# Attention step by step of one 128-query tile, with the exponentials left in PSUM

## The chip, the cores and the metric

One core of one Trainium2 chip runs the whole program. The metric is device time in microseconds; three runs of the kernel before gave a median of 1089.35 us.

## The reference

Three layers follow each other on a batch of 4 sequences of 576 tokens: attention with rotary embedding (8 heads of 64), a gated two-matrix block, and a token and channel mixer.

```python
q_rot, k_rot = (rotate(q), rotate(k))
scores = scale * np.matmul(q_rot, k_rot.transpose(0, 1, 3, 2))
scores = scores - np.max(scores, axis=-1, keepdims=True)
attn = np.exp(scores)
attn = attn / (np.sum(attn, axis=-1, keepdims=True) + 1e-09)
x = np.matmul(attn, v)
...
xk = mu_k * x + (1.0 - mu_k) * x_prev
xr = mu_r * x + (1.0 - mu_r) * x_prev
k = np.maximum(xk @ w_k, 0.0)
x = sigmoid(xr @ w_r) * (k * k @ w_v)
...
u = x + (np.maximum(x.T @ w_tok1, 0.0) @ w_tok2).T
out = u + np.maximum(u @ w_ch1, 0.0) @ w_ch2
```

## The kernel before

**Attention.** The 32 heads are worked on as 16 pairs. Of a pair, head 0 lies on partitions 0 to 63 and head 1 on 64 to 127. The 576 queries are four tiles of 128 and a last one of 64, which takes both heads at once; so a pair has nine score tiles of 128 queries by 576 keys, and the program 144. Float32 operands are split in a high and a low part, and a product is three matmuls; the keys come in two halves of 288, so a score tile is six matmuls (`emit_S`, tile `S`, two PSUM banks). VectorE takes the negative maximum (`emit_max`, `nm`), ScalarE the exponential into SBUF with the row sum (`emit_exp`, `e`), ScalarE adds the epsilon (`emit_den`, `den`), VectorE takes the reciprocal (`emit_rc`, `rc`), ScalarE writes the normalised probabilities in float16 (`emit_hi`, written by the helper `copy`, line 75, `p`), VectorE the float16 remainder (`emit_lo`, line 415), and a transposing DMA turns both into `pt` (`emit_tr`). `emit_pv` multiplies them with the split values (`pv`, 28 matmuls for each of two units of a pair), and ScalarE writes the result to `xT`.

**Steps.** `a_step(j)` runs one of five steps of a pair (`ND`), a step being a 128-query tile of both heads. It works on the exponentials of step j, the scores of j + 1 and the remainders of j - 1. In between, `other()` advances a second stream, `kvr_gen`, which computes the second layer's K and V products (`kp` in groups of 12 matmuls, `vp` in groups of 24, by `mm3`, lines 550 to 552), and `prep` rotates, splits and loads the next pair. During the first four pairs `Conv` converts weights in place of `kvr_gen`.

**Order and buffers.** What the code issues is put in order for each engine by a scheduler that follows priorities (`PRI`) and, through a timing model of its own, when operands and buffers come free; each engine then works strictly in that order. PSUM has eight banks: two score tiles of two banks (`S_p`), two banks for `pv` and the small products `vps` (`pv_p`), two for `kp` and `vp` (`acc_p`).

```python
S_p = ps.enter_context(tc.tile_pool(name="S_p", bufs=2, space=PS))
pv_p = ps.enter_context(tc.tile_pool(name="pv_p", bufs=2, space=PS))
acc_p = ps.enter_context(tc.tile_pool(name="acc_p", bufs=2, space=PS))
```

After attention the rest of the second layer, the token mixer (`trp`, `t1p`, `t2p`) and the channel mixer (`c1p`, `co`) follow.

## Time and profile before

| | before |
|---|---|
| median of 3 runs (lowest, highest) | 1089.35 us (1085.3, 1095.28) |
| the profiled execution | 1092.93 us |
| its span, first to last instruction | 1091.2 us |
| busy PE, DVE, ACT, POOL | 90%, 58%, 47%, 38% |
[...]

PE is TensorE, DVE VectorE, ACT ScalarE, POOL GpSimd. The busy shares are means over stretches with different limits, so the rows below split the span: scores run from 14 to 541 us, the last `pv` at 561 us, the channel mixer from 673 us on.

### The profile page before, as it was taken

To read this page: it belongs to the slowest core of one execution; us is meant where nothing else is said; L and a number is where in the kernel's file an instruction comes from. 1 tells how busy PE (TensorE), PEld (TensorE's weight loads), DVE (VectorE), ACT (ScalarE), POOL (GpSimd) and SP (SyncE) were. 2 spreads that over 40 slices of the span, in tenths; PEclk is the share of its full clock that TensorE was granted. 3 is DMA by queue.
4 is the path that set the end of the run, shared out by engine and by line. 5 is a ranking of instruction groups with operands and counts; after the bars stand their busy time and mean duration, and the time that the engine had idled before them with its cause. 6 is when DMAs were issued, how large, how long until landed. Compare 5 with 4: busy or idle time off the path is not lost.

```text
span 1091.2 us, 17428 instructions
## 1 busy us (share of the span) xinstructions
PE 980.3 (90%) x6544; PEld 859.3 (79%) x6544; DVE 636.8 (58%) x1098; ACT 510.2 (47%) x1160; POOL 411.9 (38%) x384
## 2 busy tenths in 40 slices
PE   2555877999999999999988799879999999999998
PEld 1443656878778777876587799879999999999998
DVE  6999986869878666761389448983223312232121
ACT  3656766767667565772455345444114212321110
POOL 5243354746758454330066355553014102201010
PEclk9955677989999999995779899889999999999999
DMA  6988698688878768573481025502021002000000
GB/s 204 251 235 168 145 192 165 151 169 172 179 157 161 166 131 157 114 163 60 97 244 70 22 61 200 230 12 55 1 66 45 23 1 65 7 22 1 23 22 22
DMA packets 212052, 120.77 MB, mean 111 GB/s; under 512 B 175232, under 2 KB 192768, under 8 KB 211840
## 3 DMA queue, kind: packets, MB, share of 16 engines
q1 hardware_dynamic: 211968, 119.67, 46.3%
q8 instruction: 51, 0.84, 0.3%
q14 instruction: 33, 0.27, 0.1%
HBM read 60.90 MB, written 14.16 MB: 69 GB/s over the span
## 4 chain that ended last, share of the span: by engine, by line
PE 67%; DVE 19%; issue 5%; DMA 4%; ACT 2%; POOL 2%; SPq 0%; DVEq 0%; POOLq 0%; ACTq 0%
PE S L368 9%; PE pv L444 6%; PE co L552 4%; PE c1p L550 4%; PE co L550 4%; PE co L551 4%; PE c1p L552 4%; PE c1p L551 4%; DVE p L415 4%; PE kp L550 4%; DVE cv L201 3%; PE kp L552 3%; PE kp L551 3%; PE vp L550 3%; PE vp L551 3%
## 5 line engine op out<-in xcount | busy, mean ns | idle before, releaser
L368 PE MATMUL S<-kq 64*128 64x288 f32 (+1 forms) x864 | 179.2, 356 | 52.8 <-ACT e L385 50.3
L368 PEld LDWEIGHTS S<-kq 64*128 64x128 f32 (+1 forms) x864 | 138.0, 221 | 85.8 <-ACT e L385 58.9
L415 DVE SCALAR_TENSOR_TENSOR p<-e,rc,p 128x576 f16<-128x576 f32 x144 | 149.2, 1058 | 23.7 <-ACT p L75 22.0
L376 DVE TENSOR_REDUCE nm<-S 128x1 f32<-128x576 f32 x144 | 107.4, 749 | 74.8 <-PE S L368 74.4
L385 ACT ACTIVATE e<-S,nm 128x576 f32<-128x576 f32 x144 | 105.8, 735 | 81.2 <-DVE nm L376 80.6
L880 DVE SCALAR_TENSOR_TENSOR hs<-c1p,hs 128x288 fp32r<-128x288 f32 x96 | 43.6, 454 | 151.3 <-ACT hs L879 151.0
L550 PE MATMUL c1p<-uhl,parts 128*128 128x288 f32 x384 | 116.5, 304 | 4.4 <-DVE hs L880 4.4
L879 ACT ACTIVATE hs<-c1p 128x288 fp32r<-128x288 f32 x96 | 38.7, 409 | 166.6 <-PE c1p L552 163.0
L551 PE MATMUL c1p<-uhl,parts 128*128 128x288 f32 x384 | 115.2, 300 | 0.0
L552 PE MATMUL c1p<-uhl,parts 128*128 128x288 f32 x384 | 114.7, 300 | 0.0
L75 ACT ACTIVATE p<-e,rc 128x576 f16<-128x576 f32 x144 | 104.1, 766 | 20.5 <-DVE rc L401 18.0
L552 PE MATMUL co<-hs,parts 128*128 128x288 f32 x384 | 113.0, 297 | 0.0
L551 PE MATMUL co<-hs,parts 128*128 128x288 f32 x384 | 113.0, 297 | 0.0
L550 PE MATMUL co<-hs,parts 128*128 128x288 f32 x384 | 109.4, 300 | 1.5 <-ACT hs L879 0.8
L104 POOL TENSOR_TENSOR k<-q,k 128x288 fp32r<-128x288 f32 x64 | 60.1, 943 | 114.6 <-DVE k L80 54.3
L104 POOL TENSOR_TENSOR uhl<-y,uhl 128x288 fp32r<-128x288 f32 x32 | 25.8, 838 | 195.2 <-ACT uhl L73 195.2
L550 PE MATMUL vp<-k,parts 128*128 128x288 f32 x256 | 84.1, 332 | 5.9 <-ACT vt L73 2.9
L444 PE MATMUL pv<-pt,vh 128*64 128x256 f16 (+1 forms) x576 | 76.4, 341 | 12.4 <-DMA pt<-p 10.7
L550 PE MATMUL kp<-xs,parts 128*128 128x288 f32 x256 | 84.8, 336 | 1.9 <-ACT t L611 1.3
L551 PE MATMUL vp<-k,parts 128*128 128x288 f32 x256 | 83.2, 326 | 0.0
L552 PE MATMUL vp<-k,parts 128*128 128x288 f32 x256 | 82.2, 322 | 0.0
L551 PE MATMUL kp<-xs,parts 128*128 128x288 f32 x256 | 81.4, 319 | 0.8 <-POOL xs L104 0.8
(113 smaller groups left out, 2409.0 us busy)
## 6 DMA issues: line engine op xcount, KB each, us to landing
words<-in_w_c_dram SPq DMA_DIRECT2D x24, 512.0 KB, 7.8
rq<-in_qin_dram SPq DMA_DIRECT2D x32, 320.0 KB, 3.3
rk<-in_kin_dram SPq DMA_DIRECT2D x32, 288.0 KB, 3.3
vr<-in_vw_dram SPq DMA_DIRECT2D x16, 320.0 KB, 3.1
xd<-xT SPq DMA_DIRECT2D x16, 288.5 KB, 2.5
vd<-vt SPq DMA_DIRECT2D x32, 144.0 KB, 2.2
y<-vd SPq DMA_DIRECT2D x8, 576.0 KB, 5.2
out_dram<-y SPq DMA_DIRECT2D x8, 576.0 KB, 3.5
```

Source lines behind the costliest of these rows:

```text
L75: act.activation(out=o, in_=i, func=AF.Copy, scale=scale)
L104: return (pool if e == "P" else dve).tensor_tensor(o, a, b, op=op)
L368: pe.matmul(ps[x][:, h, 0:HS], lhsT=a[l, 128 * m:128 * m + 128], rhs=b[l, h * HS:(h + 1) * HS], start=(n == 0), stop=(n == 2))
L376: dve.tensor_reduce(out=nm[:, x:x + 1], in_=p[:, :, 0:HS], op=ALU.max, axis=AX.XY, negate=True)
L385: act.activation(out=e, in_=p[:, :, 0:HS], func=AF.Exp, bias=sum_t[j][:, x:x + 1], accum_out=s[:, x:x + 1])
L415: dve.scalar_tensor_tensor(out=t[:, S:2 * S], in0=e_t[j][x], scalar=sum_t[j][:, x:x + 1], in1=t[:, 0:S], op0=ALU.mult, op1=ALU.subtract)
L444: pe.matmul(p[l, 0:n], lhsT=v[:, a, l], rhs=ts[x][:, c, :], start=(i == 0), stop=(i == len(prods) - 1))
L550: pe.matmul(p, lhsT=wh, rhs=t[:, 0], start=first, stop=False)
L551: pe.matmul(p, lhsT=wh, rhs=t[:, 1], start=False, stop=False)
L552: pe.matmul(p, lhsT=wl, rhs=t[:, 0], start=False, stop=last)
L879: act.activation(out=h[:, 0], in_=p[:, 0:HS], func=AF.Relu)
L880: dve.scalar_tensor_tensor(out=h[:, 1], in0=p[:, 0:HS], scalar=0.0, in1=h[:, 0].bitcast(F32), op0=ALU.max, op1=ALU.subtract)
```

## The change

A step is now one score tile instead of two heads' tiles: `ND` is 9, and the loop in `emit_S` over both heads is gone. The exponential overwrites the scores in PSUM, its row sum goes into a spare column of the same bank, and the tile stays taken until `emit_lo` has read it; before, it was free after `emit_exp`. The SBUF tile `e` and the ScalarE step `emit_den` go; VectorE adds the epsilon in a `tensor_scalar` ahead of the reciprocal. PSUM is now three score tiles, one bank for `pv` and `vps`, and one for `kp` and `vp`; only after attention (`second`) does `accps` also lend score tiles to these products. The raw loads `rk` and `rq` have four buffers instead of two, and the parts of `prep` and the `Conv` steps lie at other steps.

```diff
-ND = 5
-
-PV_AT = {4: 0, 6: 1}
+ND = 9
+
+PV_AT = {7: 0, 12: 1}
...
-BUFS = dict(rk=2, rq=2, sp=2, vr=2, v16=2, e=5, p16=4, pt=2, sm=4, sc=3, la=1, lf=1, xs=4, t=2, q=2, vt=2)
+BUFS = dict(rk=4, rq=4, sp=2, vr=2, v16=2, p16=4, pt=2, sm=4, sc=3, la=1, lf=1, xs=4, t=2, q=2, vt=2)
...
-        S_p = ps.enter_context(tc.tile_pool(name="S_p", bufs=2, space=PS))
-        pv_p = ps.enter_context(tc.tile_pool(name="pv_p", bufs=2, space=PS))
-        acc_p = ps.enter_context(tc.tile_pool(name="acc_p", bufs=2, space=PS))
+        S_p = ps.enter_context(tc.tile_pool(name="S_p", bufs=3, space=PS))
+        pv_p = ps.enter_context(tc.tile_pool(name="pv_p", bufs=1, space=PS))
+        acc_p = ps.enter_context(tc.tile_pool(name="acc_p", bufs=1, space=PS))
...
         @prio("S")
         def emit_S(j):
-            g, m = divmod(j, ND)
+            g, r = divmod(j, ND)
             (kh, kl), (qh, ql) = spl_t[g]
-            w = heads(j)
-            ps = [S_p.tile([128, 2, 512], F32, tag="S", name="S") for _ in range(w)]
+            m, x = divmod(r, 2)
+            l = slice(0, 128) if r == ND - 1 else slice(64 * x, 64 * x + 64)
+            p = S_t[j] = S_p.tile([128, 2, 512], F32, tag="S", name="S")
             for h in range(2):
                 for n, (a, b) in enumerate(((qh, kh), (qh, kl), (ql, kh))):
-                    for x in range(w):
-                        l = slice(64 * x, 64 * x + 64) if w == 2 else slice(0, 128)
-                        pe.matmul(ps[x][:, h, 0:HS], lhsT=a[l, 128 * m:128 * m + 128],
-                                  rhs=b[l, h * HS:(h + 1) * HS], start=(n == 0), stop=(n == 2))
-            S_t[j] = ps
+                    pe.matmul(p[:, h, 0:HS], lhsT=a[l, 128 * m:128 * m + 128], rhs=b[l, h * HS:(h + 1) * HS],
+                              start=(n == 0), stop=(n == 2))
...
         @prio("exp")
         def emit_exp(j):
-            s = sm_p.tile([128, 2], F32, tag="sum", name="sum")
-            e_t[j] = []
-            for x, p in enumerate(S_t.pop(j)):
-                e = e_p.tile([128, 2, HS], F32, tag="e", name="e")
-                act.activation(out=e, in_=p[:, :, 0:HS], func=AF.Exp, bias=sum_t[j][:, x:x + 1],
-                               accum_out=s[:, x:x + 1])
-                e_t[j].append(e.rearrange("p a b -> p (a b)"))
+
+            s = S_t[j][:, 0, HS:HS + 1]
+            e = S_t[j][:, :, 0:HS]
+            act.activation(out=e, in_=e, func=AF.Exp, bias=sum_t[j], accum_out=s)
             sum_t[j] = s
-
-        @prio("den")
-        def emit_den(j):
-            d = sm_p.tile([128, 2], F32, tag="den", name="den")
-            w = heads(j)
-            act.activation(out=d[:, 0:w], in_=sum_t[j][:, 0:w], func=AF.Identity, bias=eps, scale=1.0 / PSCALE)
-            sum_t[j] = d
 
         @prio("den")
         def emit_rc(j):
-            r = sm_p.tile([128, 2], F32, tag="rc", name="rc")
-            w = heads(j)
-            dve.reciprocal(r[:, 0:w], sum_t[j][:, 0:w])
+            r = sm_p.tile([128, 1], F32, tag="rc", name="rc")
+            d = sm_p.tile([128, 1], F32, tag="den", name="den")
+            dve.tensor_scalar(out=d, in0=sum_t[j], scalar1=1e-9, scalar2=1.0 / PSCALE, op0=ALU.add, op1=ALU.mult)
+            dve.reciprocal(r, d)
             sum_t[j] = r
 
         @prio("hi")
         def emit_hi(j):
-            p16_t[j] = []
-            for x, e in enumerate(e_t[j]):
-                t = p16_p.tile([128, 2 * S], F16, tag="p16", name="p16")
-                copy("A", t[:, 0:S], e, sum_t[j][:, x:x + 1])
-                p16_t[j].append(t)
+            t = p16_t[j] = p16_p.tile([128, 2, 2, HS], F16, tag="p16", name="p16")
+            copy("A", t[:, 0], S_t[j][:, :, 0:HS], sum_t[j])
 
         @prio("lo")
-        def emit_lo(j, x):
-            t = p16_t[j][x]
-            dve.scalar_tensor_tensor(out=t[:, S:2 * S], in0=e_t[j][x], scalar=sum_t[j][:, x:x + 1], in1=t[:, 0:S],
+        def emit_lo(j):
+            t = p16_t[j]
+            dve.scalar_tensor_tensor(out=t[:, 1], in0=S_t.pop(j)[:, :, 0:HS], scalar=sum_t[j], in1=t[:, 0],
                                      op0=ALU.mult, op1=ALU.subtract)
...
-            if k == -1:
+            if k == -2:
                 for n in range(3):
                     rope(g, 0, n, "DDP"[n] if g <= NP else "P")
                 ld_v(g + 1)
+            elif k == -1:
                 v_row(g)
             elif k == 0:
                 rope(g, 1, 0, "P")
@@ -474,21 +455,24 @@
                 split_hi(g, 0, "A")
                 v_pow(g)
             elif k == 1:
-                rope(g, 1, 2, "P")
-                split_lo(g, 0, "P")
                 v_all(g)
                 v_sc(g)
                 ld_raw(g + 1, 0, 0)
                 ld_raw(g + 1, 0, 1)
             elif k == 2:
+                rope(g, 1, 2, "P")
+                split_lo(g, 0, "P")
+            elif k == 3:
+                ld_raw(g + 1, 1, 0)
+                ld_raw(g + 1, 1, 1)
+            elif k == 4:
                 split_hi(g, 1, "A")
                 split_lo(g, 1, "D")
                 v_hi(g)
-                ld_raw(g + 1, 1, 0)
-                ld_raw(g + 1, 1, 1)
-            elif k == 3:
+            elif k == 5:
                 v_lo(g)
                 v_shift(g)
+            elif k == 6:
                 v_max(g + 1) if g + 1 < NG else None
...
             if j < NTT:
                 emit_exp(j)
             if j + 1 < NTT:
-                emit_S(j + 1)
+                emit_max(j + 1)
             other()
-            if j < NTT:
-                emit_den(j)
-            if j + 1 < NTT:
-                emit_max(j + 1)
             if j < NTT:
                 emit_rc(j)
                 emit_hi(j)
-            other()
             for gg in (g, g - 1):
                 r = j - gg * ND
                 if 0 <= gg < NG and r in PV_AT:
                     after.setdefault(j + 1, []).append(emit_pv(gg, PV_AT[r]))
             if 0 <= j - 1 < NTT:
-                for x in range(heads(j - 1)):
-                    emit_lo(j - 1, x)
-                    emit_tr(j - 1, x)
-                    other()
+                emit_lo(j - 1)
+                emit_tr(j - 1)
+            other()
+            if j + 2 < NTT:
+                emit_S(j + 2)
...
+
+        def accps(nm):
+            n_acc[0] += 1
+            if second and n_acc[0] % 4:
+                return S_p.tile([128, 2, 512], F32, tag="S", name=nm)[:, 0]
+            return acc_p.tile([128, 512], F32, tag="acc", name=nm)
+
+        n_acc = [0]
...
-                        p = acc_p.tile([128, 512], F32, tag="acc", name="kp")
+                        p = accps("kp")
...
-            if not cv.done() and j % 5 in (0, 2, 4):
+            if not cv.done() and j % 3 == 0:
...
-            if tps_n[0] % 3:
+            if tps_n[0] % 4:
```

The changed program orders the instructions anew. On PE, late in attention, the scores of the tile before the last pair stand among the `vp` products of the second stream. Before:

```order
L368 MATMUL S<-kq 128x288
L550 MATMUL vp<-k_5370,parts 128x288
L368 MATMUL S<-kq 128x288
L551 MATMUL vp<-k_5370,parts 128x288
L368 MATMUL S<-kq 128x288
L552 MATMUL vp<-k_5370,parts 128x288
L550 MATMUL vp<-k_5399,parts 128x288
L368 MATMUL S<-kq 128x288
L551 MATMUL vp<-k_5399,parts 128x288
L552 MATMUL vp<-k_5399,parts 128x288
L550 MATMUL vp<-k_5069,parts 128x288
```

The same place in the changed kernel:

```order
L532 MATMUL vp<-k_5378,parts 128x288
L530 MATMUL vp<-k_5422,parts 128x288
L531 MATMUL vp<-k_5422,parts 128x288
L532 MATMUL vp<-k_5422,parts 128x288
L362 MATMUL S<-kq 128x288 x18
L530 MATMUL vp<-k_5131,parts 128x288
L531 MATMUL vp<-k_5131,parts 128x288
L532 MATMUL vp<-k_5131,parts 128x288
L530 MATMUL vp<-k_5163,parts 128x288
```

The score matmuls stood one by one between single `vp` matmuls; now they stand in blocks of six or a multiple, between whole groups.

On DVE, in the middle of attention, `nm` is the maximum, `p` the remainder, `sc`, `vl`, `vm` and `kq` belong to the next pair, `f` and `k` to the second stream. Before:

```order
L415 SCALAR_TENSOR_TENSOR p_2383<-e,rc,p_2383 128x576
L540 SCALAR_TENSOR_TENSOR f<-xT,mu_s,a 128x288
L376 TENSOR_REDUCE nm<-S 128x1
L415 SCALAR_TENSOR_TENSOR p_2385<-e,rc,p_2385 128x576
L401 RECIPROCAL rc<-den 128x2
L376 TENSOR_REDUCE nm<-S 128x1
L342 SCALAR_TENSOR_TENSOR vl<-vr,sc,vh 128x640
L540 SCALAR_TENSOR_TENSOR f<-xT,mu_s,a 128x288
L415 SCALAR_TENSOR_TENSOR p_2469<-e,rc,p_2469 128x576
L415 SCALAR_TENSOR_TENSOR p_2471<-e,rc,p_2471 128x576
L376 TENSOR_REDUCE nm<-S 128x1
```

A like stretch in the changed kernel:

```order
L368 TENSOR_REDUCE nm<-S 128x1 x3
L382 TENSOR_SCALAR den<-S 128x1 x2
L383 RECIPROCAL rc<-den 128x1 x2
L382 TENSOR_SCALAR den<-S 128x1
L383 RECIPROCAL rc<-den 128x1
L394 SCALAR_TENSOR_TENSOR p_3243<-S,rc,p_3243 128x576
L394 SCALAR_TENSOR_TENSOR p_3270<-S,rc,p_3270 128x576
L340 SCALAR_TENSOR_TENSOR vl<-vr,sc,vh 128x640
L394 SCALAR_TENSOR_TENSOR p_3291<-S,rc,p_3291 128x576
L520 SCALAR_TENSOR_TENSOR f<-xT,mu_s,a 128x288
```

Maxima and remainders of two tiles used to alternate; now three maxima, three reciprocals with their `den`, and three remainders follow each other.

## Rows read from the trace of the kernel before

**Rows 1.** Busy time by stretch (start:end, length, engines, granted clock, DMA).

```profile
0.00:215.00 215.00, 138.25 (x794) 108.14 (x795) 185.78 (x315) 132.55 (x281) 98.87 (x90) 0.76 0.83 189
215.00:485.00 270.00, 267.27 (x1795) 210.25 (x1795) 197.75 (x332) 187.30 (x428) 152.68 (x126) 0.99 0.77 156
485.00:561.00 76.00, 75.90 (x334) 51.14 (x334) 28.04 (x47) 28.46 (x65) 12.13 (x13) 0.69 0.51 113
```

**Rows 2.** The same stretches, line 376 (`nm`) alone: DVE busy, count, clock, DMA.

```profile
215.00:485.00 270.00, 59.99 (x80) 0.99 0.77 156
485.00:561.00 76.00, 6.72 (x9) 0.69 0.51 113
```

**Rows 3.** Waits (waiter, releaser, us, times, longest), 485 to 561 us.

```profile
DVE nm L376 <- PE S L368: 30.6, 6, 13.2
```

**Rows 4.** Timeline of PE at full clock (start, length, what, count).

```profile
300.05 0.40 PE L552 MATMUL vp<-k,parts 128*128 128x288 f32 x1
300.38 0.30 PE L444 MATMUL pv<-pt,vh 128*64 128x256 f16 x1
300.61 0.40 PE L550 MATMUL vp<-k,parts 128*128 128x288 f32 x1
...
308.92 0.30 PE L551 MATMUL kp<-xs,parts 128*128 128x288 f32 x1
309.05 0.29 PE L552 MATMUL kp<-xs,parts 128*128 128x288 f32 x1
309.28 1.05 PE L368 MATMUL S<-kq 64*128 64x288 f32 x6
310.26 0.40 PE L550 MATMUL kp<-xs,parts 128*128 128x288 f32 x1
...
359.12 1.43 PE L368 MATMUL S<-kq 64*128 64x288 f32 x12
...
470.38 1.28 PE L444 MATMUL pv<-pt,vh 128*64 128x320 f16 x16
```

**Rows 5.** Timeline of PE at half clock.

```profile
497.06 0.61 PE L551 MATMUL vp<-k,parts 128*128 128x288 f32 x1
...
497.96 0.61 PE L552 MATMUL vp<-k,parts 128*128 128x288 f32 x1
```

**Rows 6.** The costliest groups of instructions (count, busy, mean ns, idle before and releaser).

```profile
L415 DVE SCALAR_TENSOR_TENSOR p<-e,rc,p 128x576 f16<-128x576 f32 x144 | 149.2, 1058 | 23.7 <-ACT p L75 22.0
L376 DVE TENSOR_REDUCE nm<-S 128x1 f32<-128x576 f32 x144 | 107.4, 749 | 74.8 <-PE S L368 74.4
L385 ACT ACTIVATE e<-S,nm 128x576 f32<-128x576 f32 x144 | 105.8, 735 | 81.2 <-DVE nm L376 80.6
L880 DVE SCALAR_TENSOR_TENSOR hs<-c1p,hs 128x288 fp32r<-128x288 f32 x96 | 43.6, 454 | 151.3 <-ACT hs L879 151.0
L75 ACT ACTIVATE p<-e,rc 128x576 f16<-128x576 f32 x144 | 104.1, 766 | 20.5 <-DVE rc L401 18.0
```

**Rows 7.** Instructions of single lines (count, ns min/median/max, first and last start).

```profile
L415 DVE SCALAR_TENSOR_TENSOR p<-e,rc,p x83: 786/818/2173, 214.3 to 484.9; 128x576 f16<-128x576 f32 x83
L394 ACT ACTIVATE den<-sum,eps x80: 280/295/303, 20.1 to 546.9; 128x2 f32<-128x2 f32 x64, 128x1 f32<-128x1 f32 x16
L401 DVE RECIPROCAL rc<-den x80: 130/152/167, 24.0 to 547.2; 128x2 f32<-128x2 f32 x64, 128x1 f32<-128x1 f32 x16
```

**Rows 8.** Timeline of all engines, a `kp` group's end and one score tile.

```profile
383.44 0.29 PE L552 MATMUL kp<-xs,parts 128*128 128x288 f32 x1
383.67 1.05 PE L368 MATMUL S<-kq 64*128 64x288 f32 x6
383.77 0.41 ACT L611 ACTIVATE t<-kp 128x288 f32<-128x288 f32 x1 [0.55 <-PE kp L552]
384.08 1.43 ACT L75 ACTIVATE p<-e,rc 128x576 f16<-128x576 f32 x2
...
395.51 0.80 DVE L415 SCALAR_TENSOR_TENSOR p<-e,rc,p 128x576 f16<-128x576 f32 x1
```

More of the change, by code (lines that the diff above doesn't have):

```diff
@@ L372, in emit_max @@
         @prio("max")
         def emit_max(j):
-            nm = sm_p.tile([128, 2], F32, tag="nm", name="nm")
-            for x, p in enumerate(S_t[j]):
-                dve.tensor_reduce(out=nm[:, x:x + 1], in_=p[:, :, 0:HS], op=ALU.max, axis=AX.XY, negate=True)
-            sum_t[j] = nm
+            nm = sum_t[j] = sm_p.tile([128, 1], F32, tag="nm", name="nm")
+            dve.tensor_reduce(out=nm, in_=S_t[j][:, :, 0:HS], op=ALU.max, axis=AX.XY, negate=True)
         @prio("exp")
         def emit_exp(j):
-            s = sm_p.tile([128, 2], F32, tag="sum", name="sum")
@@ L623, in kvr_gen @@
                     for m in range(KD):
-                        p = acc_p.tile([128, 512], F32, tag="acc", name="vp")
+                        p = accps("vp")
                         for kf in range(KF):
@@ L645, in kvr_gen @@
                     for m in range(KD):
-                        p = pv_p.tile([128, 512], F32, tag="pv", name="rp")
+                        p = accps("rp")
                         for kk in range(KD):
@@ L715, in body @@
         u_of, uhl_of, u_done, ch_done, M = {}, {}, set(), set(), {}
-        for j in range(4 * ND, NTT + 4):
+        for j in range(4 * ND, NTT + 5):
             a_step(j, kv.advance)
```

18 lines of the change are left out of this document (8 added, 10 removed).

## The prediction

> **What bounds the kernel now.** The view of busy time by stretch comes first, since the page's means mix three regimes. From 0 to 215 us (stage A) VectorE is busy 186 of 215 us, TensorE 138, at a mean clock of 0.76: VectorE bounds it, with the weight conversion beside the attention. From 215 to 485 us (stage B) TensorE is busy 267 of 270 us at a clock of 0.99, VectorE 198 and ScalarE 187. From 485 to 561 us (stage C) TensorE is busy throughout, at a clock of 0.69, and VectorE has little to do [rows 1]. The maxima count the tiles: 80 in B, 9 in C [rows 2], so a tile costs 270 / 80 = 3.4 us in B and 76 / 9 = 8.4 us in C. That C hangs on TensorE is seen in its waits: the maxima wait 30.6 us for scores in only 6 waits, one of 13.2 us [rows 3].
>
> A busy TensorE is not an efficient one, so the timeline comes next, read by the distance from start to start. Matmuls of one kind follow each other at 0.13 us (308.92, 309.05), sixteen `pv` take 1.28 us, 0.08 us each. But from a `vp` over one `pv` to the next `vp` it is 0.56 us (300.05 to 300.61): the alternation costs 0.56 - 0.13 - 0.08 = 0.35 us. A block of six scores among `kp` costs, from 309.05 to 310.26, 1.21 us in place of 7 x 0.13 = 0.91, so 0.30 us [rows 4]. At half clock the `vp`-`pv` round takes 0.90 us (497.06 to 497.96) [rows 5].
>
> **The change part by part: TensorE's order.** The scheduler's order decides here. From the first `kp` to the last `pv` the order before changes between `pv` and `kp`/`vp` 215 times, between scores and `kp`/`vp` 174 times; the new one 57 and 88 times. That is 79 rounds of 0.35 us and 43 of 0.30 us less: 28 + 13 = 41 us at full clock. By where they stand, 25 us of it lie in B; the rest, 16 us, in C, where single scores and `pv` alternate with `vp` for long stretches. Both stages are TensorE's, so this is on the path.
>
> **Clock in C.** A mean of 0.69 over 76 us is 52 us of work at full clock, so 24 us are lost. [...] Of the 76 us there remain 76 - 16 - 18 = 42. A check from below: nine tiles at the pace of the new B (3.2 us, below) and some 12 us for the last tile's path through `p`, transposing DMA and 28 `pv` are 41.
>
> **VectorE.** `emit_lo` now reads PSUM. It took 1058 ns in the mean but 786 at least and 818 in the median [rows 6, 7]; its long cases are those beside GpSimd, up to 2173. Of VectorE work with an operand in PSUM, line 376 takes 749 ns at the same size and line 880 454 ns at half of it [rows 6]. So 0.75 to 0.82 us; I take 0.80, nearer to the same instruction: 144 x 0.26 = 37 us less. The reciprocal, 152 ns each, grows from 80 to 144, and 144 `den` of about the same length are new: 208 x 0.152 = 32 us more [rows 7]. Net -5 us over attention (-12 to -2), 2 of it in A. It frees ScalarE instead: 80 `den` of 0.29 us are 23 us [rows 7], off the path in B and C, where ScalarE is 69% and 37% busy.
>
> [...]
>
> **ScalarE in PSUM.** No row shows ScalarE writing PSUM. `emit_exp` with a PSUM source takes 735 ns and `emit_hi` with an SBUF source 766 [rows 6]; the low end is that both take 0.73, 144 x 0.03 = 4 us less; the high end is that a pass over the same bank for reading and writing takes twice, 0.73 us more, 105 us of ScalarE. A different memory costs 4% between these rows, so I take 0.
>
> **Banks that are held longer.** The second stream has one accumulator bank instead of two, so a group's first matmul waits until ScalarE has emptied the last one. After the `kp` matmul of 383.44 (its successor starts 0.13 later) the eviction ends at 384.18: 0.61 us with ScalarE free, and up to 1.43 us more if two `emit_hi` stand ahead [rows 8]. Queued behind that wait is everything on TensorE. The new order has 63 such borders: 5 with at most one matmul in between, 13 with one block of scores (1.2 us of cover), the rest with more. I take 5 x 0.8 + 13 x 0.5 = 11 us, 9 of it in B; ends 0 and 63 x 0.9 = 57.
>
> A score tile is now held to the end of `emit_lo`. The work on it is 0.98 + 0.75 + 0.93 + 0.30 + 0.74 + 0.80 = 4.5 us, and in the new order three tiles move together, so VectorE (1.85 us per tile) serves two others meanwhile: counted along one round of three, maxima, exponentials, reciprocals, `emit_hi` and the first `emit_lo`, about 7.1 us, with the second stream's work in the queues 8.5 to 9, or 2.8 to 3.0 us per tile. TensorE's new need in B is (270 - 25 + 9) / 80 = 3.2 us. It stays the later one, narrowly; taken 0.
>
> **Paired scores.** Scores of two heads, alternated, can run side by side: twelve at 359.12 end after 1.43 us, six at 309.28 after 1.05 [rows 4]. The new loop ends that. In the timeline 35 of 384 possible pairs start together, 22 of them in A: 13 x 0.13 = 2 us on the path, 5 more in A beside VectorE. [...]
>
> **Stage A.** VectorE's net is -2 us. Slots held to `emit_lo` can leave it idle, and the doubled `rk`/`rq` buffers spare GpSimd waits: 0, with -15 to +20. **Second stream.** At the last `pv` 1056 of its matmuls are done instead of 1100: 44 x 0.13 = 6 us later. What follows 561 us I move along unchanged.
>
> **Sum.** B: -25 + 9; C: -34 + 2; pairs +2, VectorE in A -2, second stream +6: -42 us. From the profiled execution, 1092.9 us, which lies 3.6 above the median of 1089.35, this gives 1051; against the median I say **1047 us**.
>
> **The rivals.** *More:* the slots prove ample and A gains too. A 0.3 us faster per tile over 54 tiles and B another 0.2 over 80: 16 + 16 us, 1015. For it speaks that ScalarE and VectorE are unsaturated in B; against, that VectorE stays busy in A. *Same:* the one accumulator bank gives back what the order saves: at 0.7 us for each of 63 borders, 44 instead of 11 us, 1080; against it speaks the cover in the order. *Slower:* the held score tiles become the bound. One tile now takes from 383.67 to 396.31, 12.6 us, from its first score to the end of `emit_lo` [rows 8]; the place is the fourth score block, which must wait for that end. From a hold of 3 x 3.2 = 9.6 us on it decides. At 11.5 us a tile costs 3.8 us in B and C, 89 x 0.6 = 53 us, and in A some 10 more: 1110. Against it: in the old order nothing hurried `emit_lo`; the new order puts it ahead of the next maxima. *Exponential in place slow:* at +0.73 us, a round of three grows by about 2.2 us, above TensorE's need by some 0.5 us per tile over 144: 72 us, 1119; only the high end does this. *Pairing lost in full:* all 384 pairs instead of 13 on the path, +48 us, 1095; the 35 pairs exclude it nearly. [...] *It does not do what it says:* the end of attention moves, but what follows waits for its own weight conversion: 1085; against it, that conversion can only start once attention's SBUF is given back.
>
> **How the numbers follow.** Forecast 0.54 (1026 to 1071), more 0.18, same 0.08, slower 0.10, slow exponential 0.05, pairing 0.01, not moved 0.04. Leaving out half of the first rival and most of the last ones' upper parts, the range is 1010 to 1100. About 1% is what a measurement of this kernel can tell from no change: faster by more 0.72, within 1% 0.13, slower 0.15.
>
> **What would show it.** In the changed kernel the last `pv` should start near 520 us instead of 561; `vp` and `pv` should no longer alternate; the stretch around the last ten tiles should show a clock near 1. Line 394 should take 0.75 to 0.82 us without long cases, the exponential 0.74, `emit_hi` 0.73 to 0.77. The waits of `kp` and `vp` for ScalarE show the accumulator's price, and those of scores for `emit_lo` the held tiles; more than some 30 us of either in B would make the prediction wrong, as would a first 54 tiles that end past 235 us.

## The result: 1049 us after 1092

| | before | after |
|---|---|---|
| median beside each other (4 runs each) | 1092.32 us | 1049.05 us |
| ratio, 95% interval | | 0.9603, 0.9533 to 0.9674 |
| the profiled execution, its span | 1092.93, 1091.2 us | 1050.36, 1048.6 us |
| maximum of tile 54 starts (end of A) | 213 us | 230 us |
| maximum of tile 135 starts (end of B) | 489 us | 486 us |
| last `pv` starts (end of C) | 561.3 us | 527.3 us |
| `kp` and `vp` matmuls started by then | 1100 | 1056 |
| last `pv` to last `co` | 524.5 us | 516.0 us |

Tiles are counted from 0. Three of the four runs after took 1045.99 to 1050.36 us at a mean granted TensorE clock of 0.93 to 0.95, 1 being full clock; the fourth, of 1082.97 us at 0.81, was disturbed and does not count in the ratio.

**By stages.** Busy time by stretch in the changed kernel, cut at its own stages (columns as in [rows 1]: length, then PE, PEld, DVE, ACT, POOL with their instructions, the granted clock, the DMA share and GB/s):

```profile
0.00:230.00 230.00, 130.91 (x768) 102.12 (x769) 188.65 (x383) 122.16 (x245) 116.57 (x98) 0.83 0.77 186
230.00:486.00 256.00, 244.36 (x1844) 209.99 (x1842) 203.67 (x476) 180.78 (x399) 125.84 (x121) 0.95 0.83 167
486.00:528.00 42.00, 36.09 (x276) 31.08 (x275) 29.45 (x67) 26.10 (x62) 9.96 (x12) 0.96 0.81 168
528.00:1048.00 520.00, 496.69 (x3663) 488.33 (x3661) 206.92 (x384) 156.41 (x377) 139.25 (x154) 0.98 0.16 54
```

C takes 42 us at a clock of 0.96 where it took 76 at 0.69 [rows 1] (72 us from tile 135 on); B handles 81 tiles in 256 us, 3.16 us each, where it was 3.4. A has become longer, and the reason can be read in its first row: VectorE is busy 189 us, 3 more than before, but of 230 instead of 215: it stands idle for 41 us where it was 29. So the change loses 17 us in A, wins 20 in B (276 to 256, from tile 54 to tile 135) and 31 in C, and 8.5 behind the last `pv`.

**TensorE's order.** The timeline of PE late in attention, the place of [rows 5] (start, length, line, what; in brackets the idle time ahead of it and what ended it):

```profile
489.13 0.30 PE L531 MATMUL vp<-k,parts 128*128 128x288 f32 x1
489.27 0.29 PE L532 MATMUL vp<-k,parts 128*128 128x288 f32 x1
489.77 1.03 PE L362 MATMUL S<-kq 64*128 64x288 f32 x6 [0.21 <-DVE p L394]
491.77 0.40 PE L530 MATMUL vp<-k,parts 128*128 128x288 f32 x1 [0.96 <-ACT vt L73]
492.01 0.29 PE L531 MATMUL vp<-k,parts 128*128 128x288 f32 x1
```

Groups of `vp` run at 0.13 us from start to start, then six scores in a block (489.77), then the next group. Nothing alternates. The prices of the change stand there as well: 0.21 us in which the score block waits for `emit_lo` (line 394) to give a score tile back, and 0.96 us in which the next `vp` waits for ScalarE (`vt`) to empty the one accumulator bank.

**The steps of a tile.** The costliest groups from 0 to 528 us (busy us, mean ns of one, idle before and what ended it), the counterpart of [rows 6, 7]:

```profile
L394 DVE SCALAR_TENSOR_TENSOR p<-S,rc,p 128x576 f16<-128x576 f32 x144 | 113.7, 809 | 15.0 <-ACT p L75 13.9
...
L368 DVE TENSOR_REDUCE nm<-S 128x1 f32<-128x576 f32 x144 | 106.4, 749 | 32.7 <-PE S L362 32.3
...
L75 ACT ACTIVATE p<-S,rc 128x576 f16<-128x576 f32 x144 | 104.2, 751 | 18.0 <-ACT S L375 5.8 <-DVE rc L383 4.7 <-issue 4.2
...
L375 ACT ACTIVATE S<-S,nm 128x576 f32<-128x576 f32 x144 | 102.3, 715 | 73.6 <-DVE nm L368 72.3 <-DVE va L309 0.5
...
L383 DVE RECIPROCAL rc<-den 128x1 f32<-128x1 f32 x144 | 22.2, 158 | 2.7
...
L382 DVE TENSOR_SCALAR den<-S 128x1 f32<-128x1 f32 x144 | 21.1, 148 | 14.7 <-ACT S L375 13.7
```

`emit_lo` takes 809 ns from PSUM, 786 to 819 in all 144 cases. The exponential in place takes 715 ns where it took 735 into SBUF, and `emit_hi` 751 reading PSUM where it took 766 reading SBUF.

**Waits.** Three answers of the view of waits (engine, line, releaser: us in all, times, longest us). The first 175 us:

```profile
PE S L362 <- DVE p L394: 34.2, 10, 9.8
...
PE pv L424 <- DMA pt<-p: 18.0, 10, 4.7
```

From 230 to 486 us, PE alone:

```profile
PE S L362 <- DVE p L394: 2.1, 4, 1.1
...
PE vp L530 <- ACT vt L73: 1.5, 3, 0.9
PE kp L530 <- ACT t L599: 0.8, 2, 0.5
```

From 486 to 528 us, PE alone:

```profile
PE kp L530 <- ACT t L599: 4.7, 4, 2.0
PE vp L530 <- ACT vt L73: 1.0, 1, 1.0
```

The wait of the score block for `emit_lo` is 34.2 us of the first 175 in ten long waits, and 2.1 us of stage B. By itself it does not show why A grew: in the same 175 us of the kernel before TensorE waited longer, for the exponential to give a score tile back,

```profile
PE S L368 <- ACT e L385: 44.9, 20, 6.1
```

and in A it is VectorE that bounds. The accumulator bank costs 1.5 + 0.8 us in B and 4.7 + 1.0 in C.

### The profile page after: what moved, and what is told of

It is laid out like the page before. It is cut to its first block, busy times and chain, and to the rows that moved or that the text cites. A ratio compares the mean times of both kernels' runs of the same rounds, so it can differ in the third digit from the quotient of the medians.

```text
span 1048.6 us, 17649 instructions
## 1 busy us (share of the span) xinstructions
PE 908.0 (87%) x6544; PEld 831.5 (79%) x6544; DVE 628.7 (60%) x1306; ACT 485.5 (46%) x1080; POOL 391.6 (37%) x383
## 4 chain that ended last, share of the span: by engine, by line
PE 48%; DVE 10%; issue 2%; DMA 2%; POOL 2%; ACT 1%; SPq 0%; DVEq 0%; POOLq 0%; ACTq 0%
PE c1p L530 5%; PE c1p L531 5%; PE c1p L532 5%; PE co L531 5%; PE co L530 4%; PE co L532 4%; PE S L362 3%; DVE cv L196 2%; DVE cv L200 2%; DVE cv L202 2%; PE vp L530 2%; PE vp L531 1%; PE vp L532 1%; PE pv L424 1%; PE rp L530 1%
## 5 line engine op out<-in xcount | busy, mean ns | idle before, releaser
L362 PE MATMUL S<-kq 64*128 64x288 f32 (+1 forms) x864 | 153.0, 346 | 49.7 <-DVE p L394 39.0
L362 PEld LDWEIGHTS S<-kq 64*128 64x128 f32 (+1 forms) x864 | 125.1, 219 | 73.6 <-issue 39.5
L375 ACT ACTIVATE S<-S,nm 128x576 f32<-128x576 f32 x144 | 102.3, 715 | 73.6 <-DVE nm L368 72.3
L394 DVE SCALAR_TENSOR_TENSOR p<-S,rc,p 128x576 f16<-128x576 f32 x144 | 113.7, 809 | 15.0 <-ACT p L75 13.9
L75 ACT ACTIVATE p<-S,rc 128x576 f16<-128x576 f32 x144 | 104.2, 751 | 18.0 <-ACT S L375 5.8
L104 POOL TENSOR_TENSOR k<-q,k 128x288 fp32r<-128x288 f32 x64 | 54.4, 852 | 123.2 <-DVE k L80 85.0
L530 PE MATMUL kp<-xs,parts 128*128 128x288 f32 x256 | 82.9, 331 | 12.2 <-ACT t L599 6.6
L530 PE MATMUL vp<-k,parts 128*128 128x288 f32 x256 | 79.6, 313 | 3.8 <-ACT vt L73 3.0
L424 PE MATMUL pv<-pt,vh 128*64 128x256 f16 (+1 forms) x576 | 59.4, 334 | 26.1 <-DMA pt<-p 24.5
L530 PEld LDWEIGHTS c1p<-uhl,parts 128*128 128x128 f32 x384 | 73.4, 192 | 7.7 <-DVE hs L869 4.3
L531 PE MATMUL kp<-xs,parts 128*128 128x288 f32 x256 | 78.6, 309 | 0.7 <-POOL xs L104 0.6
L531 PE MATMUL vp<-k,parts 128*128 128x288 f32 x256 | 78.2, 307 | 0.5 <-POOL k L104 0.5
```

What stands on the lines that cost most here:

```text
L75: act.activation(out=o, in_=i, func=AF.Copy, scale=scale)
L104: return (pool if e == "P" else dve).tensor_tensor(o, a, b, op=op)
L362: pe.matmul(p[:, h, 0:HS], lhsT=a[l, 128 * m:128 * m + 128], rhs=b[l, h * HS:(h + 1) * HS], start=(n == 0), stop=(n == 2))
L375: act.activation(out=e, in_=e, func=AF.Exp, bias=sum_t[j], accum_out=s)
L394: dve.scalar_tensor_tensor(out=t[:, 1], in0=S_t.pop(j)[:, :, 0:HS], scalar=sum_t[j], in1=t[:, 0], op0=ALU.mult, op1=ALU.subtract)
L424: pe.matmul(p[l, 0:n], lhsT=v[:, a, l], rhs=ts[x][:, c, :], start=(i == 0), stop=(i == len(prods) - 1))
```

## The experiments

The question was which part of the change makes the gain. **Theory:** TensorE's order alone, with the clock that follows from it; the exponentials in PSUM bring nothing by themselves. **Rivals:** the exponentials in PSUM (shorter `emit_lo`, ScalarE freed of `den`); the third score tile; the lending of banks after attention. A ratio below is against the kernel before run beside it.

**1. The kernel before, with another priority for the second stream's matmuls alone.**

```diff
-... rope=200, conv1=20, kv=-200, kvpe=-200)
+... rope=200, conv1=20, kv=-200, kvpe=-2000)
```

> The kernel before with one number changed: the products of the second stream get a priority lower by 1800, so that they no longer slip between pv matmuls. In its order pv and kp/vp change 55 times instead of 215, scores and kp/vp 123 times instead of 174; steps, banks, exponentials in SBUF and the 1100 matmuls of the second stream by the last pv stay. If TensorE's order is the cause: 80 rounds x 0.35 + 25 x 0.30 = 35 us less, and some 18 more where the clock no longer falls near the end of attention, so a ratio of 0.95 to 0.97. If the one-tile step or the exponentials in PSUM are the cause: 1.00.

The number moves `kp` and `vp` behind the scores and `pv` in the scheduler's order: from the first `kp` to the last `pv` the order changes 55 times between `pv` and `kp`/`vp` (before 215), 123 times between scores and `kp`/`vp` (174); an order with few such changes is called calm below. Measured: **1043.61 us, 0.9648 (0.9568 to 0.9729)**, last `pv` at 510.3 us. Busy time by stretch, the counterpart of B and C:

```profile
215.00:470.00 255.00, 250.08 (x1814) 208.44 (x1813) 201.57 (x331) 186.21 (x428) 146.10 (x125) 0.98 0.84 168
470.00:511.00 41.00, 39.88 (x316) 33.43 (x315) 28.71 (x47) 26.98 (x61) 13.47 (x13) 1.00 0.84 188
```

81 tiles in B took 259 us and C 40, at 0.98 and 1.00 of full clock. One number in the kernel before buys what the rewritten attention buys. The exponentials went to SBUF, ScalarE kept its `den`, and banks and steps were the old ones.

**2. The kernel before, with a higher priority for `pv`.**

```diff
-PRI = dict(den=50, hi=400, pv=20, ...
+PRI = dict(den=50, hi=400, pv=400, ...
```

> The kernel before with the priority of pv raised from 20 to 400: pv and kp/vp change 34 times instead of 215, scores and kp/vp 133 times instead of 174, and the second stream stands at 1170 matmuls instead of 1100 at the last pv. Order as the cause: 90 x 0.35 + 20 x 0.30 = 38 us and the clock, 0.95 to 0.97. The other causes: 1.00.

34 and 133 changes; **1047.89 us, 0.9676 (0.9612 to 0.974)**; last `pv` at 524.5 us with 1170 of the stream's matmuls done. A second, different way to a calm order gives nearly the same time.

**3. The changed kernel with the old banks: two score tiles, two `pv`, two accumulators.**

```diff
-        S_p = ps.enter_context(tc.tile_pool(name="S_p", bufs=3, space=PS))
-        pv_p = ps.enter_context(tc.tile_pool(name="pv_p", bufs=1, space=PS))
-        acc_p = ps.enter_context(tc.tile_pool(name="acc_p", bufs=1, space=PS))
+        S_p = ps.enter_context(tc.tile_pool(name="S_p", bufs=2, space=PS))
+        pv_p = ps.enter_context(tc.tile_pool(name="pv_p", bufs=2, space=PS))
+        acc_p = ps.enter_context(tc.tile_pool(name="acc_p", bufs=2, space=PS))
```

> The changed kernel with the old banks: two score tiles, two banks for pv, two for kp/vp. Its order is as calm as that of the changed kernel (pv and kp/vp change 37 times). If held score tiles bound stage A (0 to the 54th tile), that stage grows by half, from 230 to 270 us or more, and the whole is 30 to 80 us slower than the changed kernel, slower than or equal to the kernel before. If the slots do not matter and only the order does: 0.95 to 0.97, and less waiting of kp for ScalarE.

**1165.38 us, 1.076 (1.0691 to 1.0828)**, with an order as calm as any (37 and 106 changes). The largest wait of PE over the whole span:

```profile
PE S L362 <- DVE p L394: 99.1, 24, 14.3
```

99 us wait for `emit_lo`, and the 81 tiles of B take 326 us. The whole is 116 us slower than the changed kernel, where 30 to 80 were expected. A tile in place in PSUM is held through `nm`, exponential, `den`, `rc`, `emit_hi` and `emit_lo`; with two slots that bounds the kernel. The third slot does not bring the gain, but in this form the exponentials in PSUM can't do without it.

**4. The changed kernel with the exponentials written to SBUF again**, its nine steps and its three score tiles kept. The raw loads go back to two buffers, to make room for the tiles `e`.

```diff
-BUFS = dict(rk=4, rq=4, sp=2, vr=2, v16=2, p16=4, ...
+BUFS = dict(rk=2, rq=2, sp=2, vr=2, v16=2, e=4, p16=4, ...
...
-            s = S_t[j][:, 0, HS:HS + 1]
-            e = S_t[j][:, :, 0:HS]
-            act.activation(out=e, in_=e, func=AF.Exp, bias=sum_t[j], accum_out=s)
+            s = sm_p.tile([128, 1], F32, tag="sum", name="sum")
+            e = e_p.tile([128, 2, HS], F32, tag="e", name="e")
+            act.activation(out=e, in_=S_t[j][:, :, 0:HS], func=AF.Exp, bias=sum_t[j], accum_out=s)
...
+            S_t[j] = e
```

> The changed kernel with the exponentials and row sums in SBUF again (four tiles e, and for their room two rk and rq buffers): a score tile is free after the exponential. Its order is calm (pv and kp/vp change 44 times). If the held tiles cost stage A its 17 us, the 54th tile comes back to 205 to 216 us, the rest of attention stays as in the changed kernel, and the ratio is 0.935 to 0.95. If the order of the weight conversion costs them, the 54th tile stays near 230 us and the ratio at 0.96 to 0.97. If the exponentials in PSUM themselves bring the gain: 0.98 to 1.00, and the long remainders on VectorE (up to 2.1 us beside GpSimd) are back in any case.

**1046.98 us, 0.9666 (0.9599 to 0.9732)**. Busy time by stretch, cut at tile 54, at tile 135 and at the last `pv`:

```profile
0.00:199.00 199.00, 120.72 (x708) 95.21 (x710) 185.29 (x378) 122.35 (x238) 81.59 (x76) 0.73 0.82 192
199.00:448.00 249.00, 227.33 (x1736) 197.11 (x1733) 212.99 (x443) 171.61 (x374) 162.13 (x125) 0.95 0.84 172
448.00:491.00 43.00, 41.92 (x358) 35.91 (x357) 24.51 (x62) 26.72 (x60) 12.40 (x14) 1.00 0.84 165
491.00:1042.00 551.00, 520.52 (x3748) 510.36 (x3748) 232.88 (x426) 172.15 (x411) 157.06 (x169) 0.95 0.17 59
```

Tile 54 comes at 199 us instead of 230, with VectorE busy 185 of the 199; that is the 17 us which the changed kernel lost in A, and 14 more. VectorE's idle time there is 14 us instead of 41, at about the same work: both kernels have done 64 of the VectorE instructions that convert weights. (TensorE has done 44 fewer of the second stream's matmuls, some 6 us.) B takes 249 us and the last `pv` comes at 490.5 instead of 527.3. But attention outruns the second stream: 972 of its matmuls are done by then instead of 1056, and the stretch to the end grows from 516 to 546 us. So attention ends 37 us sooner when a tile is let go after the exponential (some 11 of them are the 84 matmuls not done, at 0.13), and it is paid back behind it, where 139 of the converting instructions are left instead of 104, 110 us of VectorE instead of 84. The time is the same with the exponentials in SBUF and in PSUM, and the ratio of 0.935 to 0.95 that was expected if held tiles cost A its 17 us did not come. The raw loads' buffers were not tried apart, nor the order, which the edit changes on every engine.

**5. The kernel before, with the lending of score banks after attention.** **6. The changed kernel without it.** **7. Experiment 1 with it.** The edit of 5 and 7 is the function `accps` of the change and its three calls, of which one stands here; then that of 6:

```diff
-                        p = acc_p.tile([128, 512], F32, tag="acc", name="kp")
+                        p = accps("kp")
```

```diff
-            if second and n_acc[0] % 4:
+            if False:
```

> The kernel before; only after attention three of four kp, vp and rp products borrow a score bank, as in the changed kernel. Nothing ahead of the last pv moves, so that stays at 561 us. Theory: the lending is what shortened the stretch from the last pv to the end (524.5 us before, 516 after); it gives 516 here too, 1081 us or 0.992 of the time before. Rival: that stretch shrank for another reason (which weights are converted by then, or the lending of score banks to the token mixer's products out of three slots); then 524 us, 1087, ratio 1.00.

> The changed kernel without the lending: all kp, vp and rp products use the one accumulator bank also after attention. Ahead of the last pv (527 us) nothing moves. Theory: the lending hides the evictions there; without it each of the 100 or so products after attention waits for ScalarE, at 0.1 to 0.6 us each 10 to 60 us, so the stretch to the end grows from 516 to 530 us or more, 1063 us or more, ratio to the kernel before 0.975. Rival: evictions are hidden behind the token mixer's own matmuls; 516 us, 1049, ratio 0.96.

> The kernel before with both the lower priority of the second stream's matmuls (which alone gave 1043.6 us, last pv at 510, 524.4 us from there to the end) and the lending after attention. Theory: the two add up, the stretch after the last pv shrinks by 8 to 14 us: 1030 to 1036 us, ratio 0.953 to 0.958, below the changed kernel. Rival: the lending brings nothing without the third score slot: 1044, ratio 0.965.

Measured: 5: 1084.37 us, **0.9997 (0.9943 to 1.005)**; last `pv` to last `co` 525.2 us, nothing won. 6: 1076.07 us, **0.9958 (0.9905 to 1.001)**; 541.3 us, 25 more than in the changed kernel. 7: 1044.85 us, **0.9633 (0.9568 to 0.9698)**; nothing won over experiment 1. The theory of 5 and that of 7 fell, that of 6 held: lending saves nothing where there are two accumulator banks, and it mends a loss where there is one. From 528 us on, without lending:

```profile
528.00:680.00 152.00, 122.17 (x779) 111.76 (x779) 79.85 (x129) 59.17 (x134) 66.98 (x73) 0.92 0.29 103
680.00:1074.00 394.00, 384.46 (x2885) 381.45 (x2885) 127.70 (x256) 98.70 (x244) 72.56 (x80) 0.99 0.10 32
```

and the changed kernel over the same stretch:

```profile
528.00:680.00 152.00, 134.71 (x918) 128.13 (x916) 111.47 (x174) 70.12 (x157) 80.45 (x82) 0.93 0.33 120
680.00:1048.00 368.00, 361.98 (x2747) 360.20 (x2745) 95.45 (x211) 86.29 (x220) 58.80 (x73) 1.00 0.09 27
```

TensorE is busy 122 of 152 us without lending and 135 with it. So most of the gain hangs on a part of the change that stands behind attention.

Run 5 shows something else that was not looked for. Its order on TensorE is that of the kernel before up to the last tiles, yet C ran at full clock:

```profile
485.00:550.00 65.00, 64.03 (x390) 46.65 (x389) 34.95 (x57) 32.60 (x74) 14.67 (x15) 1.00 0.68 154
```

From the first single score of C the same 231 matmuls (54 scores, 84 `pv`, 93 `vp` and `kp`) took 60.8 us in the profile of the kernel before and 43.6 in this one. TensorE is busy in 60.8 of 60.8 us of the first stretch and in 64.03 of 65 in the row above, at a granted clock of 0.65 and of 1.00: the difference, 17.2 us, goes with the clock. The kernel before does not pay it in every execution: beside runs 5 to 8 it took 1074 to 1097 us in 19 runs, at a mean granted clock of 0.93 to 0.95 in the five below 1079 us and of 0.90 to 0.91 in the seven above 1094. So 1049 us is 2.4% less than the best of these and 4.4% less than the worst; the profile of the kernel before less the 17.2 us gives 1075.7, about its best executions. With a calm order the times lie closer: 1042 to 1048 in run 1, 1046 to 1050 in three of the four runs of the changed kernel.

**8. The kernel before, with one bank for `pv` and `vps`.**

```diff
-        pv_p = ps.enter_context(tc.tile_pool(name="pv_p", bufs=2, space=PS))
+        pv_p = ps.enter_context(tc.tile_pool(name="pv_p", bufs=1, space=PS))
```

> The kernel before with one bank for pv and vps in place of two, and nothing else. The scheduler's order from the first kp to the last pv then changes between pv and kp/vp 54 times instead of 215, and between scores and kp/vp 111 instead of 174; 1149 matmuls of the second stream are done by the last pv instead of 1100. Theory that the order makes the time: 40 us and the clock's 15 to 20 are saved as with the low priority, 49 more matmuls ahead of the last pv take 6 us there and give them back behind it; last pv near 518 us, 1045 to 1050 us, ratio 0.96 to 0.965. Rival: the single bank makes each of the 32 pv units and 32 vps wait for the eviction of the last, 0.6 to 1.4 us each, 20 to 45 us given back: 1065 to 1090, ratio 0.98 to 1.0.

**1043.94 us, 0.9623 (0.9552 to 0.9694)**; last `pv` at 515.9 us. Taking a bank away makes the kernel faster: the scheduler's order comes out calm (54 and 111 changes), and the waits that the rival put at 20 to 45 us are not there: all that is listed for TensorE from 215 to 516 us is 6.7 us. This is a part of the change that suffices by itself.

**9. The matmuls alone.** The core of a kernel of which only TensorE runs; `w`, `x`, `vh`, `pt` lie ready, and a dependency keeps the order as written.

```python
def vp(p, i, n):
    then(pe.matmul(p[:, 0:HS], lhsT=w, rhs=x, start=(i == 0), stop=(i == n - 1)))
def pv(p, i, n):
    then(pe.matmul(p[L[i % 2], 0:256], lhsT=vh[:, L[i % 2]], rhs=pt, start=(i < 2), stop=(i >= n - 2)))
def s0(p, i, n):
    then(pe.matmul(p[:, 0:HS], lhsT=w[L[0], :], rhs=x[L[0], :], start=(i == 0), stop=(i == n - 1)))
```

> Leaves out the whole computation (the output is zeros and one row of products): only TensorE runs, on operands that lie ready, in sections of 64 rounds behind a warm-up of 512. Forms as in the kernel: 128 x 288 on 128 x 128 weights (vp), 256 columns in float16 on 128 x 64 weights (pv), 288 columns on 64 rows (a score). Theory: the price lies in the change of kind itself, so a round vp, pv takes 0.56 us at full clock as in the kernel before, of which 0.35 is for the two changes; in blocks of four and four the same 0.35 once per block, 4 x 0.21 + 0.35 = 1.19; a round vp, score 0.13 + 0.13 + 0.30 = 0.56, in blocks of eight 16 x 0.13 + 0.30 = 2.4. Two more sections change one thing at a time, the narrow weights (still four-byte) and the type (still 128 wide), and show which of the two pays. Rival: the 0.56 us in the kernel were waits for operands or banks that the trace does not name; then a round vp, pv takes 0.21 us here, and blocks change nothing.

At full clock, from start to start: `vp` alone 0.132 us, `pv` alone 0.053 (two halves of the columns side by side in 0.106). The timeline of the section that alternates them:

```profile
100.46 0.40 PE L63 MATMUL alt_p<-x,w 128*128 128x288 f32 x1
100.78 0.30 PE L66 MATMUL alt_q<-pt,vh 128*64 128x256 f16 x1
101.01 0.40 PE L63 MATMUL alt_p<-x,w 128*128 128x288 f32 x1
```

A round is 100.46 to 101.01, 0.55 us, where [rows 4] show 0.56, and here there is nothing to wait for. The price of alternating is 0.553 - 0.132 - 0.053 = 0.37 us. In blocks of four and four a block pair took 1.06 us, 0.74 for the matmuls and 0.32 for the two changes. Four-byte matmuls on 64 columns alternated with `vp` at hardly any price:

```profile
145.00 0.29 PE L63 MATMUL narrow_p<-x,w 128*128 128x288 f32 x1
145.13 0.28 PE L72 MATMUL narrow_q<-x,w 128*64 128x256 f32 x1
145.25 0.29 PE L63 MATMUL narrow_p<-x,w 128*128 128x288 f32 x1
```

0.25 us a round; float16 on all 128 columns took 0.26. That leaves 0.12 and 0.13 for the second matmul, which has 256 columns where `vp` has 288; it was not timed alone. Scores on 64 rows alternated with `vp` cost 0.65 us a round, 0.39 more than two at 0.132; 4.9 us into that section the granted clock fell to 0.5. It stayed there through 35 us of blocks of eight and 15 us of scores alone, and rose only in the last section. Two scores on different rows, the last section, started within 0.02 us of each other, a pair every 0.13 us.

**12. Which change pays, and when the clock falls.** The same frame with other sections.

```python
sec("low", vp, pvl)               # pv always in the first 64 columns
sec("high", vp, pvh)              # always in the second
sec("pair", vp, pv, blk=2)
sec("rows", vp, s0, n=16)         # 16 rounds, a score on the first 64 rows
sec("upper", vp, s1, n=16)        # on the second
sec("rowblock", vp, s0, blk=8)    # eight and eight
sec("rowlong", vp, s0)            # 64 rounds; 128 vp lie between the last sections
```

> Leaves out the whole computation, as in the run of the matmuls alone, where a round vp, pv took 0.55 us at full clock (0.132 + 0.053 by themselves), while four-byte matmuls on 64 columns and float16 ones on 128 columns alternated with vp at no price, and the clock fell 5 us after vp and scores on 64 rows began to alternate. Here: vp alternated with pv always in the first 64 columns, then always in the second, then two and two (one of each half); vp alternated with a score on the first and on the second 64 rows, 16 rounds each, with 128 vp in between; blocks of eight and eight; and 64 rounds of vp and single scores at the end. Theory that the price is for moving to another part of the array: the first 64 columns cost nothing (0.24 us a round), the second 0.55; rows first 0.26, second 0.65. Rival, that any tile narrower than 128 in float16 pays: 0.55 in both, and 64 rows pay 0.39 in both. On the clock: if single scores between single vp let it fall, it falls in the last section and not in the one of 16 rounds, nor in blocks of eight; if it was chance, it stays.

Busy time by stretch, inside the sections low, rows (its first 6 us, then its end), rowblock, and rowlong:

```profile
74.00:109.00 35.00, 35.00 (x129) 18.43 (x127) 0.00 (x0) 0.00 (x0) 0.00 (x0) 1.00 0.00 0
...
184.00:190.00 6.00, 6.00 (x21) 3.38 (x19) 0.00 (x0) 0.00 (x0) 0.00 (x0) 1.00 0.00 0
191.00:196.00 5.00, 5.00 (x11) 2.74 (x10) 0.00 (x0) 0.00 (x0) 0.00 (x0) 0.50 0.00 0
248.00:268.00 20.00, 20.00 (x132) 17.54 (x131) 0.00 (x0) 0.00 (x0) 0.00 (x0) 1.00 0.00 1
...
290.00:350.00 60.00, 60.00 (x113) 31.99 (x112) 0.00 (x0) 0.00 (x0) 0.00 (x0) 0.50 0.00 0
```

Low and high both take 0.55 us a round, and 64 rows 0.65 in either half; blocks of two took 0.69 us for a pair of blocks (0.32 for its changes), and eight `vp` with eight scores 2.49 (0.38). The price is the same in either half, and the first theory fell. In float16 a tile of 64 columns pays (0.55 us a round), in four bytes it hardly does (0.25), and a four-byte tile of 64 rows pays (0.65). The weight loads look different: in the section low they are busy 18 of 35 us and TensorE is the whole time, while in the warm-up of `vp` alone (experiment 9) they are busy 69.3 of 69.5 us. No run shows whether the price comes from there.

The granted clock fell from 1.00 to 0.50 in every section of single scores between single `vp`, here after 6.4, 5.6 and 4.0 us, and in experiment 9 after 4.9; so already in the sections of 16 rounds, sooner than was expected. It stayed at 1.00 in three times 35 us of `vp` and `pv`, and in 20 us of blocks of eight. The timeline of the section rows:

```profile
184.23 0.40 PE L78 MATMUL rows_q<-x,w 64*128 64x288 f32 x1
184.56 0.40 PE L63 MATMUL rows_p<-x,w 128*128 128x288 f32 x1
...
190.11 0.39 PE L78 MATMUL rows_q<-x,w 64*128 64x288 f32 x1
190.44 0.61 PE L63 MATMUL rows_p<-x,w 128*128 128x288 f32 x1
190.97 0.61 PE L78 MATMUL rows_q<-x,w 64*128 64x288 f32 x1
```

The distance from start to start goes from 0.33 to 0.53 us at 190.44. The kernel before does the same at the edge of C. Its PE timeline there:

```profile
488.25 0.40 PE L368 MATMUL S<-kq 64*128 64x288 f32 x1
488.58 0.40 PE L551 MATMUL vp<-k,parts 128*128 128x288 f32 x1
488.91 0.39 PE L368 MATMUL S<-kq 64*128 64x288 f32 x1
489.24 0.40 PE L552 MATMUL vp<-k,parts 128*128 128x288 f32 x1
489.57 0.42 PE L444 MATMUL pv<-pt,vh 128*64 128x256 f16 x1
489.92 0.61 PE L550 MATMUL vp<-k,parts 128*128 128x288 f32 x1
```

Six single scores between `vp` begin at 485.24, the last two stand in these rows, and from 489.57 on the distances are those of half clock (granted 0.50 from 489.6 to 517). In C it fell twice, at 489.5 and at 530.5 us, the second time behind single scores again (526.8 to 528.5). The same scores at 490.4 to 494.1 in run 5 were not followed by a fall (1.00 from 485 to 550 us), so it need not happen: in the kernel there are six such rounds, two of them with two or three `vp`.

**10. The changed kernel with the second stream ahead.** **11. The kernel before with one `pv` bank and three accumulator banks.**

```diff
-... kv=-200, kvpe=-200)
+... kv=-200, kvpe=300)
```

```diff
-        pv_p = ps.enter_context(tc.tile_pool(name="pv_p", bufs=2, space=PS))
-        acc_p = ps.enter_context(tc.tile_pool(name="acc_p", bufs=2, space=PS))
+        pv_p = ps.enter_context(tc.tile_pool(name="pv_p", bufs=1, space=PS))
+        acc_p = ps.enter_context(tc.tile_pool(name="acc_p", bufs=3, space=PS))
```

> The changed kernel with a higher priority for the second stream's matmuls; its order changes as seldom (53 times between pv and kp/vp, 92 between scores and kp/vp), but 1179 instead of 1056 of the stream's matmuls are done by the last pv. Theory: TensorE bounds both sides of that point, so 123 matmuls of 0.13 us move 16 us from behind it to ahead of it; last pv near 543 us, the total unchanged at 1049, ratio 0.96 (the term of 6 us for 44 fewer of them was then no gain and no loss). Rival: they fill TensorE's idle time in attention, some 12 us in stage B and 6 in C; then 1037 to 1043, ratio 0.95.

> The kernel before with one bank for pv and vps (1043.9 us by itself) and the freed bank given to kp and vp, three in place of two. Order as calm (54 and 124 changes), 1179 of the stream's matmuls by the last pv. Theory: with two accumulator banks evictions are hidden already; 1042 to 1046 us, ratio 0.96 to 0.965. Rival: accumulator borders still cost some 0.1 us or more each at the 60 borders in attention and 60 behind it; then 1030 to 1036, ratio 0.95, the best of all.

10: **1052.86 us, 0.9791 (0.9755 to 0.9827)** beside a kernel before that took 1074 to 1078 in most of its runs. Its last `pv` is at 545.5 us, 18 later than in the changed kernel, and the stretch behind it is 16 shorter: 123 matmuls moved across, the theory's 16 us, and nothing won. 11: **1036.65 us, 0.9643 (0.9606 to 0.9681)** beside the same runs, 1034 to 1041 in all four. It lies under both kernels: 16 us under run 10 on the same chip, and all its runs under all of the changed kernel's, though those were timed beside other runs of the kernel before, so that difference of 12 us is less certain than the one of 16. B and C in its profile:

```profile
215.00:470.00 255.00, 253.34 (x1890) 212.99 (x1888) 203.78 (x341) 188.20 (x440) 150.95 (x128) 1.00 0.86 174
470.00:513.00 43.00, 42.16 (x343) 37.58 (x337) 30.13 (x52) 28.05 (x67) 13.03 (x14) 1.00 0.73 164
```

TensorE is busy 253 of 255 and 42 of 43 us, at full clock. The rival of 11, that borders at the accumulator still cost something with two banks, gains some 7 us from the step from run 8 to run 11, which ran on different chips; by their ratios, 0.9623 and 0.9643, it gains nothing. This is not told apart.

## Why the prediction was right, and where not

The forecast was 1047 us and the sign, the place and most of the sum came out. By its own steps:

- **TensorE's order, 41 us: right, and a little small.** Experiments 9 and 12 give the two prices by themselves, 0.37 and 0.39 us a round instead of 0.35 and 0.30: 79 x 0.37 + 43 x 0.39 = 46 us. That they are prices of the order and not waits was an assumption, and experiment 9 shows it; that the order moves the time without the one-tile step or the exponentials in PSUM is shown by experiments 1, 2 and 8.
- **Clock in C, 18 of 24 us: right in size.** No run shows the 18 as such, which was the author's estimate; in its place the same 231 matmuls cost 17.2 us more at the fallen clock. As to where it falls, the runs narrow it down: it fell from 1.00 to 0.50 in all four sections of single scores on 64 rows and in none of the three of single `pv`. Run 5, with the same order and 1.00 throughout C, shows that in the kernel such scores are not always followed by a fall.
- **B, -25 + 9 = -16: -20 measured.** The mis-sized term is the accumulator's border there, 9 us: B waited 2.3. In C it waited 5.7 where 2 was put. Together 8 instead of 11. That B came out near is in part luck. Between tiles 54 and 135 the order changes 41 times instead of 146 between `pv` and `kp`/`vp` and 67 instead of 128 between scores and `kp`/`vp`, which at the measured prices is 31 us, not 25. Against that stand two things for which the sum had no term: TensorE is idle for 12 us of B (244 busy of 256) where it was 3, and the granted clock stands at half for 24 us of B, in five stretches, where it did for 7.
- **VectorE, -5: the parts are right.** `emit_lo` at 0.809 us against 0.80 assumed, `den` and `rc` at 148 and 158 ns against 152. The 809 ns from PSUM are below the median of 818 that the same operation took from SBUF [rows 7].
- **ScalarE in PSUM, 0: right.** 20 and 15 ns less, 144 x 0.035 = 5 us of an engine that bounds nothing; the high end of +105 us is excluded.
- **Paired scores, +2: not measured apart.** The last section of experiment 9 shows two scores side by side; no run restores the pairs in the changed kernel.
- **Held score tiles, 0: right in B (2.1 us), wrong in A.** Stage A stood at -2 us with pairs beside it, and its range reached +20: it took 17 more. The step that failed is "slots held to `emit_lo` can leave it idle", put at 0: VectorE's idle time in A went from 29 to 41 us. In A the conversion of weights shares VectorE, `emit_lo` queues behind it, and ten waits of 3.4 us in the mean held the next scores back. Experiment 4 speaks for it, by letting the tile go: -31 us to tile 54, and 14 us idle. It does not prove it, since the kernel before waited still longer for its exponentials (44.9 us), and since VectorE itself waits only 10.9 us for scores up to tile 54 where it waited 8.3; which waits carry the 17 us stays open. Experiment 3 shows the rival of held tiles in full, at 1165.
- **Second stream, +6: right as a price.** Run 10 moved 123 matmuls for 16 us and won nothing.
- **What follows 561, unchanged: wrong twice, in opposite directions.** Counting the 44 matmuls left over, the stretch should have been 530 us. On the one accumulator bank without lending it is 541 (run 6), 11 more; the lending takes off 25, to 516; neither was in the sum. The 14 us under 530 are not explained by lending alone (run 5). In the changed kernel each of the four VectorE steps that convert a weight is left 26 times behind the last `pv` instead of 32 or 33 times, 84 us of VectorE instead of 105. Nor is this enough alone: counted to 1100 matmuls of the second stream, the stretch is 510 us in the changed kernel and in run 10, but 526 in run 3, where as few conversions are left (82 us) but two score tiles are lent beside two accumulator banks, and 529 in run 4, with three tiles and 110 us left. The cause was not tried by itself and stays open.

So the total was within 2 us of the forecast partly by luck: +17 in A, -14 behind attention and some smaller misses cancelled.

## What to carry to other kernels

Before attention's memory layout is rewritten, look at TensorE's timeline from start to start: an engine that is busy throughout may spend two thirds of a stretch on changes between kinds of matmul (0.37 of 0.55 us), and one priority or one bank less can order them in blocks. Count a buffer's whole hold at the place where its consumer is most loaded, not where it is least; and when a bank is taken away, follow the change to the end of the program, where the same bank serves other products. A gain against a kernel whose clock falls in some executions should be read against its best executions too.
